# Attention and soft mixture of experts: the upper part of k by a transfer, epsilon and a running sum on ScalarE, halved casts, one routing step to a round

## The chip, the cores and the metric

The kernel runs on one core of a Trainium2 chip. The time is that of one execution on the device, in microseconds. It is the median of several runs; the profile is of one further execution.

## The reference

Attention for 8 batches of 12 heads (448 positions, 64 values per head), then a soft mixture of 8 experts with 4 slots each. Cut to what matters:

```python
scores = scale * np.matmul(q, k.transpose(0, 1, 3, 2))          # causal mask follows
scores = scores - np.max(scores, axis=-1, keepdims=True)
attn = np.exp(scores)
attn = attn / (np.sum(attn, axis=-1, keepdims=True) + 1e-09)
x = np.matmul(attn, v)                                            # then (3584, 768)
logits = x @ phi                                                  # (3584, 32)
d = np.exp(logits - logits.max(0)); d /= d.sum(0) + 1e-09         # over all tokens
slot_input = d.T @ x
slot_out[e] = np.maximum(slot_input[e] @ w1[e], 0.0) @ w2[e]
c = softmax(logits, over slots)
out = c @ slot_out
```

## The kernel before

The attention stage works in rounds, one per head: 96 rounds, two to a pair of heads, 12 to a batch (a block). Each round is software-pipelined. In round `i`, TensorE makes the scores of head `i+2` (`scores1`: matmuls `s<-tri` for the mask and `s<-qd,ks`), adds corrections and the negated row maximum to the scores of head `i` (`scores2`: `s<-r,k`), and multiplies the exponentials of head `i-1` by the values (`attv`: `po<-va,pt`). One `po` bank serves all heads; three banks hold scores.

q and k are held in two parts. `cast_k` and `cast_q` round the raw `qk` tile into `ks` and `qd` on ScalarE. `sub_k` and `sub_q` put the remainders into partitions 64 to 127 of `ks` and `r2` on GpSimd (`ks<-qk,ks`, `r<-qk,qd`). `copy_k2` copies the rounded (upper) part of k from partitions 0 to 63 of `ks` to partitions 64 to 127 of `k2`, which the corrections take as weights (`k<-ks` in the profile). The tiles `qd`, `ks`, `k2` and `r2` exist twice, for even and odd pairs.

The row maximum goes over several engines. ScalarE evacuates a piece of the scores (`max_evac`, `mx<-s`). VectorE takes the maximum with the rest, transposes and reduces (`mx<-s,mx`, `mt<-mx`, `r<-mt`). TensorE transposes the result (`rt<-ident,r`) into the one bank `m`, VectorE reduces it (`mr<-rt`), and GpSimd spreads it (`r<-mr`). ScalarE makes the exponentials (`exps`, `pt<-s`), which frees a bank of scores. `norm` divides: step 0 adds epsilon to the row sums (`sm<-po`), step 1 takes the reciprocal, step 2 multiplies (`x<-po,sm`), which frees `po`.

At the end of a round, `plan` runs a step of the routing, if there is one:

- `xtrans` transposes `x` of a pair (`xt<-ident,x`, copied out by ScalarE as `xts<-xt`).
- `next_logits` multiplies two pairs by `phi` (`g<-xts,phi`).
- `logits_e` transposes exponentials and logits (`tp`), copies them, and calls `logits_z`, which updates the running sum `run_z`.
- `dispatch` multiplies `x` by the exponentials (`sp<-x,gs`).

Each of these takes the same one bank `m` as `rt`. `logits_d` (`ld` in the table) makes the routing exponentials `gs` and the factor `al` on ScalarE, once a block.

The order within a round is written out by hand in `ORDER`, one list for even and one for odd rounds. Every engine works in the order of the program. Loads go out on SP's queue in program order, at the head of an odd round: k, v, q, and in every second pair a tile of expert weights. After attention come the expert stage and the combination, which run against the stream of expert weights.

Of the kernel before, what the change touches and what calls it, by code (L numbers as in the profile page):

```python
# [9 lines left out]
F32 = mybir.dt.float32  # L10
F32R = mybir.dt.float32r
BF16 = mybir.dt.bfloat16
AF = mybir.ActivationFunctionType
ALU = mybir.AluOpType
# [3 lines left out]
P = 128  # L18
NB, NH, S, HD = 8, 12, 448, 64
# [8 lines left out]
EPS = 1e-9  # L28
# [3 lines left out]
NR, XB = 2, 3  # L32
# [7 lines left out]


ORDER = (
# [4 lines left out]
)  # L47

SC0, SC1, SC2, SC3 = 512, 0, 320, 960
# [30 lines left out]
def attention_soft_moe(ctx: ExitStack, tc: tile.TileContext, qk, va, phi, w1, w2, out):  # L80
    nc = _Core(tc)
    const = ctx.enter_context(tc.tile_pool(name="const", bufs=1, side="left"))
# [27 lines left out]
    st = {}  # L110
# [54 lines left out]
    k2_, r2_ = ([t[k] for t in ops] for k in range(2))  # L165
    po0 = ps_1.tile([P, NCH, VC], F32, name="po")
    identb = const.tile([P, P], BF16, name="identb")
    nc.vector.tensor_copy(out=identb, in_=ident)
    for i in range(NR):
        nc.gpsimd.memset(r2_[i][0:64, :, :].bitcast(F32), 0.0)  # L170
# [5 lines left out]
    def misc(name):  # L176
        return ps_1.tile([P, 512], F32, tag="m", name=name)
# [9 lines left out]
    def cast_q(p, hs=slice(0, 2)):  # L187
        if p < NPAIR:
            nc.scalar.activation(out=qd_[p % NR][:, hs], in_=st["raw", 0, p][:, hs], func=AF.Copy)

    def cast_k(p, hs=slice(0, 2)):
        if p < NPAIR:
            nc.scalar.activation(out=ks_[p % NR][:, hs], in_=st["raw", 1, p][:, hs], func=AF.Copy)

    def sub_k(p, hs=slice(0, 2), eng=None):
        if p < NPAIR:
            ks = ks_[p % NR][64:P, hs]
            (eng or nc.gpsimd).tensor_tensor(out=ks, in0=st["raw", 1, p][64:P, hs], in1=ks, op=ALU.subtract)

    def copy_k2(p, hs=slice(0, 2)):  # L200
        if p < NPAIR:
            nc.scalar.activation(out=k2_[p % NR][64:P, hs], in_=ks_[p % NR][0:64, hs],
                                 func=AF.Copy)

    def sub_q(p, hs=slice(0, 2), eng=None):
        if p < NPAIR:
# [107 lines left out]
    def norm(i, k):  # L314
        if not 0 <= i < NHD:
            return
        p, h = divmod(i, 2)
        if k == 0:
            if i % 6 == 0:
                xn = x_[p // 3 % XB]  # L320
                st["xn", p // 3] = xn
                for k in range(3):
                    st["x", p + k] = xn[:, :, P * k:P * k + P]
            sm = st["sm", i] = moe.tile([P, NCH], F32, tag="sm", name=f"sm{i}", bufs=2)
            nc.vector.tensor_scalar(out=sm, in0=st.get(("po", i), po0)[:, :, HD], scalar1=EPS, scalar2=None, op0=ALU.add)
        elif k == 1:
            nc.vector.reciprocal(out=st["sm", i], in_=st["sm", i])
        else:
            sm = st.pop(("sm", i))
            nc.vector.tensor_tensor(out=st["x", p][:, :, HD * h:HD * h + HD], in0=st.get(("po", i), po0)[:, :, 0:HD],  # L330
                                    in1=sm.unsqueeze(2).to_broadcast([P, NCH, HD]), op=ALU.mult)
# [12 lines left out]
    def logits_a(b, js, g, first=True, last=True):  # L344

        for j in js:
            xt = st.pop(("xt", b * PPB + j))
            for c in range(NCH):
                nc.tensor.matmul(g[32 * c:32 * c + 32], phis[j // 3][:, j % 3], xt[:, P * c:P * c + P],
                                 start=first and j == js[0], stop=last and j == js[-1], skip_group_check=True)  # L350

    def logits_t(j, g):

        nc.vector.tensor_tensor(out=lt, in0=g, in1=lt if j else mk, op=ALU.add)
# [15 lines left out]
    def logits_z(b):  # L370
        nc.vector.scalar_tensor_tensor(out=run_z, in0=run_z, scalar=st["al", b][:, 0:1],
                                       in1=st.pop(("bs", b)), op0=ALU.mult, op1=ALU.add)

    def logits_e(b):
        tp = misc(f"tp{b}")
        nc.tensor.transpose(out=tp[:, 0:P], in_=gs, identity=ident)
        nc.tensor.transpose(out=tp[:, P:2 * P], in_=lt, identity=ident)
        st["dn", b] = gs.rearrange("p (c s) -> p c s", s=NSLOT)
        nc.scalar.activation(out=gs, in_=tp[:, 0:P], func=AF.Copy)
        nc.scalar.activation(out=lg[:, b], in_=tp[:, P:2 * P], func=AF.Copy)  # L380
        logits_z(b)

    def dispatch_a(b, hf, sp, sl=slice(0, 384)):
        dn = st["dn", b]
# [9 lines left out]
                                       op0=ALU.mult, op1=ALU.add)  # L394


    def first_logits(b, m):
        logits_a(b, (0, 1), m[:, 384:512], first=b == 0)
        logits_t(0, m[:, 384:512])

    def next_logits(b, j, m):
        logits_a(b, (j, j + 1), m[:, 0:P])
        logits_t(j, m[:, 0:P])

    def dispatch(b, hf):
        sp = misc(f"sp{b}_{hf}")
        dispatch_a(b, hf, sp)
        if hf:

            first_logits(b + 1, sp)  # L410
        dispatch_b(b, hf, sp)

    plan = {}
    for b in range(NB):
        o, last = 12 * b, b == NB - 1
        for j, r in enumerate((3, 5, 8, 9, 11, 13)):
            if not last or j < PPB - 2:
                plan[o + r] = lambda p=b * PPB + j: xtrans(p)
        plan[o + 10] = lambda b=b: next_logits(b, 2, misc(f"g{b}_2"))
        if not last:  # L420
            plan[o + 14] = lambda b=b: (next_logits(b, 4, misc(f"g{b}_4")), logits_b(b, lt))
            plan[o + 16] = lambda b=b: logits_e(b)
            plan[o + 18] = lambda b=b: dispatch(b, 0)
            plan[o + 19] = lambda b=b: dispatch(b, 1)
    plan[7] = lambda: first_logits(0, misc("g0_0"))


    warm(START[0])
# [57 lines left out]
    for i in range(NHD + 1):  # L486
        p, h = divmod(i, 2)
        if h:
            load_qk(p + 3, 1)
            if p + 1 < NPAIR - 1:  # L490
                loads_v(p + 1)
            load_qk(p + 3, 0)
            if p % 2 and nload < RES:
                load_w(nload)
                nload += 1
        if i == NHD - 3:

            loads_v(NPAIR - 1, nc.scalar)
        if i < 2:
            scores2(i, (1, 0, 2))  # L500
            if i:
                scores1_all(3)
                max_evac(3)
            scores2(i, (3,))
            exps(i)
            if i == 0:
                max_row(1, 0)
                max_row(1, 1)
                max_spread(1)
                sub_q(1, h1)  # L510

        qs = [int(n[1]) for n in ORDER[h] if n[0] == "a"]
        first = qs[:2] if qs[0] == 3 else qs[:1]
        for n in ORDER[h]:
            if i < 2 and (n in ("ev", "exp") or n[0] in "kt" or n in ("c0", "c3", "c12")):
                continue
            if i == 0 and n in ("mr0", "mr1", "sp"):
                continue
            if n[0] == "k" or n in ("c0", "c3", "c12"):
                scores1(i + 2, n)  # L520
            elif n[0] == "t":
                scores2(i, (int(n[1]),))
            elif n[0] == "a":
                attv(i - 1, (int(n[1]),), first)
            elif n[0] == "x":
                max_keys(i + 2, int(n[1]))
            elif n[0] == "n":
                norm(i - 1, int(n[1]))
            elif n in ("mr0", "mr1"):
                max_row(i + 1, int(n[2]))  # L530
            elif n == "ld":
                if i % 12 == 3 and i > 12:
                    logits_d(i // 12 - 1, lt)
            elif n == "plan":
                if later and i:
                    later.pop(0)()
                plan.get(i, int)()
            else:
                {"ev": lambda: max_evac(i + 2), "exp": lambda: exps(i), "sp": lambda: max_spread(i + 1),
                 "ck": lambda: cast_k(p + 2), "sk": lambda: sub_k(p + 2), "cq": lambda: cast_q(p + 2),  # L540
                 "c2": lambda: copy_k2(p + 1), "sq": lambda: sub_q(p + 2)}[n]()
        if i == NHD - 1:

            scs.close()
            pe = att.enter_context(tc.tile_pool(name="pe", bufs=1, space=PSUM, reuse_waits="tile"))
            ps = [pe.tile([P, 512], F32, name=f"e{k}") for k in range(6)]
            po = st["po", i] = ps[2][:, 0:NCH * VC].rearrange("p (c n) -> p c n", n=VC)
# [259 lines left out]
```

## Time and profile before

| | us |
|---|---|
| median of 3 runs | 463.79 (463.17 to 464.12) |
| profiled execution | 461.8, span 460.1 |
| TensorE matmul busy | 426.2 (93%) |
| VectorE busy | 354.2 (77%) |
| ScalarE busy | 329.7 (72%) |
| GpSimd busy | 266.1 (58%) |

Busy time is an average over the attention stage (to about 355 us) and the expert stage. In the rows of a timeline the first number is the start in microseconds from the start of the span, the second the time that the row covers; a row with `x10` merges ten neighbouring instructions. In rows of groups, the numbers behind `x47 |` are busy microseconds and the mean nanoseconds of one.

### The profile page before, as it was taken

How to read it: one execution, taken by the hardware profiler on the slowest of the kernel's cores; microseconds unless marked ns; L12 is line 12 of the kernel's file. 1: busy time of each engine (PE TensorE's matmuls, PEld its weight loads, DVE VectorE, ACT ScalarE, POOL GpSimd, SP SyncE). 2: the span in 40 equal slices, each digit the busy share in tenths (PEclk: the TensorE clock that was granted, in tenths of full speed). 3: DMA queues.
4: the chain of work that ended last, by engine and by line, in shares of the span. 5: the costliest groups of instructions: out<-in, count | busy, mean ns of one | idle time of the engine just before them, and what ended most of it. 6: DMA issues, size and time to landing. Idle time of an engine off the chain costs nothing.

```text
span 460.1 us, 12026 instructions
## 1 busy us (share of the span) xinstructions
PE 426.2 (93%) x4581; PEld 363.3 (79%) x4581; DVE 354.2 (77%) x1051; ACT 329.7 (72%) x489; POOL 266.1 (58%) x215
## 2 busy tenths in 40 slices
PE   7899999999999999999999999999999998996640
PEld 3799999999899989998999899999989754542220
DVE  5888899888988988898899888988897468422340
ACT  6798888889888979987889788888985211332230
POOL 5888788677778777877777687777772000000000
PEclk9999999999999999999999999999999999999985
DMA  7376666676567765776566766667648999999998
GB/s 267 112 273 236 222 205 219 225 234 219 191 205 255 234 211 173 236 251 217 192 209 217 233 234 206 214 215 236 227 158 285 374 407 413 416 414 414 401 395 301
DMA packets 38200, 119.03 MB, mean 259 GB/s; under 512 B 4096, under 2 KB 11776, under 8 KB 38144
## 3 DMA queue, kind: packets, MB, share of 16 engines
q1 hardware_dynamic: 38000, 118.01, 73.1%
q8 instruction: 36, 0.59, 0.5%
q10 hardware_dynamic: 144, 0.27, 0.1%
q14 instruction: 20, 0.16, 0.1%
HBM read 107.25 MB, written 11.01 MB: 257 GB/s over the span
## 4 chain that ended last, share of the span: by engine, by line
PE 68%; DMA 14%; DVE 6%; ACT 5%; issue 3%; POOL 1%; SPq 0%; ACTq 0%; POOLq 0%
PE po L64 29%; PE s L64 23%; DMA w<-in_w_dram 13%; PE xt L64 5%; PE sp L64 3%; PE g L64 2%; ACT pt L64 2%; PE rt L64 2%; ACT ks L64 2%; DVE mx L64 1%; PE e L64 1%; PE pp L64 1%; DMA qk<-in_qk_dram 1%; DVE run_z L64 1%; PE hp L64 1%
## 5 line engine op out<-in xcount | busy, mean ns | idle before, releaser
L64 PE MATMUL po<-va,pt 128*128 128x65 f32 x1900 | 193.5, 250 | 0.0
L64 PEld LDWEIGHTS po<-va,pt 128*128 128x128 f32 x1900 | 190.5, 171 | 0.3 <-DVE x L64 0.2
L64 DVE TENSOR_TENSOR mx<-s,mx 128x320 f32<-128x320 f32 (+2 forms) x288 | 100.8, 350 | 28.2 <-ACT mx L64 24.6
L64 POOL TENSOR_TENSOR r<-qk,qd 64x896 fp32r<-64x896 f32 (+1 forms) x50 | 101.4, 2028 | 6.6 <-ACT qd L64 2.8
L64 POOL TENSOR_SCALAR_AFFINE_SELECT r<-mr 14x448 fp32r<-14x448 f32 x96 | 61.4, 640 | 75.6 <-DVE mr L64 67.6
L64 ACT ACTIVATE pt<-s 128x1024 f32<-128x1024 f32 x96 | 98.0, 1021 | 7.4 <-PE s L64 3.8
L64 POOL TENSOR_TENSOR ks<-qk,ks 64x896 fp32r<-64x896 f32 (+1 forms) x47 | 98.0, 2085 | 5.1 <-ACT ks L64 1.5
L64 PE MATMUL s<-r,k 128*128 128x320 f32 (+3 forms) x384 | 83.1, 298 | 1.8 <-POOL r L64 1.7
L64 PE MATMUL s<-qd,ks 128*128 128x448 f32 (+3 forms) x384 | 77.3, 312 | 1.1 <-DVE ks L64 1.1
L64 ACT ACTIVATE mx<-s 128x448 f32<-128x448 f32 x96 | 52.4, 546 | 34.5 <-PE s L64 17.3
L64 PEld LDWEIGHTS s<-r,k 128*128 128x128 f32 (+1 forms) x384 | 60.0, 176 | 5.9 <-POOL r L64 2.2
L64 DVE STREAM_TRANSPOSE mt<-mx 128x448 f32<-128x448 f32 x96 | 61.9, 645 | 3.3
L64 DVE TENSOR_REDUCE r<-mt 128x14 f32<-128x448 f32 x96 | 58.5, 609 | 0.1
L64 PEld LDWEIGHTS s<-qd,ks 128*128 128x128 f32 (+1 forms) x384 | 55.8, 182 | 2.6 <-ACT qd L64 1.8
L64 ACT ACTIVATE ks<-qk 128x896 fp32r<-128x896 f32 (+1 forms) x50 | 45.6, 914 | 2.8 <-DMA qk<-in_qk_dram 2.8
L64 ACT ACTIVATE k<-ks 64x896 fp32r<-64x896 f32 (+1 forms) x49 | 45.8, 934 | 1.1
L64 ACT ACTIVATE qd<-qk 128x896 fp32r<-128x896 f32 (+1 forms) x50 | 46.1, 922 | 0.4 <-DMA qk<-in_qk_dram 0.3
L64 PEld LDWEIGHTS <-identb 128*128 128x128 bf16 x320 | 29.5, 102 | 18.5 <-issue 14.8
L64 DVE TENSOR_TENSOR x<-po,sm 128x256 f32<-128x256 f32 x95 | 40.3, 425 | 3.3
L64 PE MATMUL s<-tri,identb 128*128 128x64 bf16 (+2 forms) x288 | 40.0, 235 | 0.9
L64 ACT ACTIVATE xts<-xt 128x512 f32<-128x512 f32 x47 | 28.1, 598 | 9.0 <-PE xt L64 6.0
L64 PE MATMUL so<-w,ht 128*32 128x384 f32 x256 | 24.9, 492 | 6.9 <-DMA w<-in_w_dram 5.2
(126 smaller groups left out, 398.1 us busy)
## 6 DMA issues: line engine op xcount, KB each, us to landing
w<-in_w_dram SPq DMA_DIRECT2D x64, 768.0 KB, 8.0
qk<-in_qk_dram SPq DMA_DIRECT2D x94, 448.0 KB, 3.4
va<-in_va_dram SPq DMA_DIRECT2D x47, 260.0 KB, 3.4
out_dram<-ot SPq DMA_DIRECT2D x28, 384.0 KB, 6.7
qk<-in_qk_dram SPq DMA_DIRECT2D x4, 224.0 KB, 3.6
va<-in_va_dram ACTq DMA_DIRECT2D x1, 260.0 KB, 4.8
phi<-in_phi_dram SPq DMA_DIRECT2D x2, 48.0 KB, 3.8
```

Source lines behind the costliest of these rows:

```text
L64: return self._tc.keep_in_program_order(op(*args, **kwargs))
```

## The change

- `copy_k2` becomes a transfer from SBUF to SBUF on SP's queue, except for the first pair, and moves from the end of an odd round to the head of the next even one in the list, where it serves the pair `p + 1` a round earlier.
- Step 0 of `norm` and the update of `run_z` run on ScalarE.
- k and q are cast by single heads: k in the even round (one head at its head, one before the exponential), q in the odd round (before, both heads of both were cast in the even round).
- The first logits of a block leave the second dispatch and become a step of their own at round 8; some transposes move by a round.

```diff
-    ("c3", ..., "t3", "ck",
-     "mr0", "exp", "x0", "a2", "mr1", "x2", "x3", "a1", "cq", "sp", "n0", ...),
-    ("c3", ..., "a3", "exp", "mr0", ..., "sq", "c2", "x4", "plan"),
+    ("c2", "ck0", "c3", ..., "t3", "ck1",
+     "mr0", "exp", "x0", "a2", "mr1", "x2", "x3", "a1", "sp", "n0", ...),
+    ("cq0", "c3", ..., "a3", "cq1", "exp", "mr0", ..., "sq", "x4", "plan"),
...
+    eps = const.tile([P, 1], F32, name="eps")
+    nc.gpsimd.memset(eps, EPS)
...
+            if p < 1:
+                nc.scalar.activation(out=k2_[p % NR][64:P, hs], in_=ks_[p % NR][0:64, hs],
+                                     func=AF.Copy)
+            else:
+                nc.sync.dma_start(out=k2_[p % NR][64:P, hs].bitcast(F32),
+                                  in_=ks_[p % NR][0:64, hs].bitcast(F32))
...
-            nc.vector.tensor_scalar(out=sm, in0=st.get(("po", i), po0)[:, :, HD], scalar1=EPS, ...)
+            nc.scalar.activation(out=sm, in_=st.get(("po", i), po0)[:, :, HD], func=AF.Identity, bias=eps[:, 0:1])
...
-        logits_z(b)
+        nc.scalar.activation(out=run_z, in_=run_z, func=AF.Identity, scale=st["al", b][:, 0:1],
+                             bias=st.pop(("bs", b))[:, 0:1])
...
         dispatch_a(b, hf, sp)
-        if hf:
-
-            first_logits(b + 1, sp)
         dispatch_b(b, hf, sp)
...
-        for j, r in enumerate((3, 5, 8, 9, 11, 13)):
+        for j, r in enumerate((3, 5, 9, 10, 12, 13)):
...
-        plan[o + 10] = lambda b=b: next_logits(b, 2, misc(f"g{b}_2"))
+        for j, r in ((0, 8), (2, 11)):
+            plan[o + r] = lambda b=b, j=j: next_logits(b, j, misc(f"g{b}_{j}"))
...
-    plan[7] = lambda: first_logits(0, misc("g0_0"))
```

ScalarE, an even round with a transposed pair at its start, in the fifth block. `k_125` is `k2`, `qk_25` the raw tiles of pair 25, `mx` the evacuation and `pt` the exponential. Before:

```order
L64 ACTIVATE pt_87<-s_2443 128x1024
L64 ACTIVATE k_125<-ks_122 64x896
L64 ACTIVATE xts_2599<-xt_2594 128x512
L64 ACTIVATE mx<-s_2601 128x448
L64 ACTIVATE ks_122<-qk_25_2548 128x896
L64 ACTIVATE pt_85<-s_2499 128x1024
L64 ACTIVATE qd_121<-qk_25_2551 128x896
```

Now:

```order
L64 ACTIVATE pt_87<-s_2491 128x1024
L64 ACTIVATE sm_2631<-po,eps 128x4
L64 ACTIVATE xts_2643<-xt_2638 128x512
L64 ACTIVATE ks_122<-qk_25_2591 128x448
L64 ACTIVATE mx<-s_2647 128x448
L64 ACTIVATE ks_122<-qk_25_2591 128x448
L64 ACTIVATE pt_85<-s_2540 128x1024
L64 ACTIVATE sm_2681<-po,eps 128x4
```

The copy of k is gone ahead of `xts`, the epsilon has come there, one half of the cast of k stands ahead of `mx`, and the cast of q is no longer in this round.

TensorE, from the second dispatch of a block (`sp_1`) to the end of the round after it. Before, with the first logits behind the dispatch and a transpose in the next round:

```order
L64 MATMUL sp_1_2484<-x_91,gs 32x384 x4
L64 MATMUL sp_1_2484<-xts_2285,phi_221 32x128 x4
L64 MATMUL sp_1_2484<-xts_2386,phi_221 32x128 x4
L64 LDWEIGHTS identb
L64 MATMUL s_2499<-tri,identb 128x64
```

```order
L64 MATMUL rt_2519<-ident,r_2482 14x128
L64 MATMUL po<-va_86,pt_87 128x65 x5
L64 MATMUL xt_2541<-ident,x_90 128x128 x4
L64 LDWEIGHTS identb
L64 MATMUL s_2553<-tri,identb 128x64
```

Now, the end of that next round:

```order
L64 MATMUL rt_2560<-ident,r_2530 14x128
L64 MATMUL po<-va_86,pt_87 128x65 x5
L64 MATMUL g_0_2581<-xts_2329,phi_223 32x128 x4
L64 MATMUL g_0_2581<-xts_2432,phi_223 32x128 x4
L64 LDWEIGHTS identb
L64 MATMUL s_2597<-tri,identb 128x64
```

The logits stand in a round of their own, and the transposes follow a round later.

SP's queue, now (`k_125` is `k2`, `va` the values, `w` a tile of expert weights):

```order
L64 DMA qk_12_1200<-in_qk_dram 128x896
L64 DMA w_1202<-in_w_dram 128x1536
L64 DMA k_125<-ks_122 64x896
L64 DMA qk_13_1305<-in_qk_dram 128x896
L64 DMA va_86<-in_va_dram 128x520
L64 DMA qk_13_1308<-in_qk_dram 128x896
```

The transfer is new in its third row; the other rows stand as before.

More of the change, by code (lines that the diff above doesn't have):

```diff
@@ L201, in copy_k2 @@
         if p < NPAIR:
-            nc.scalar.activation(out=k2_[p % NR][64:P, hs], in_=ks_[p % NR][0:64, hs],
-                                 func=AF.Copy)
+            if p < 1:
[4 more added lines that the diff above has]
+                                  in_=ks_[p % NR][0:64, hs].bitcast(F32))
     def sub_q(p, hs=slice(0, 2), eng=None):
@@ L324, in norm @@
             sm = st["sm", i] = moe.tile([P, NCH], F32, tag="sm", name=f"sm{i}", bufs=2)
-            nc.vector.tensor_scalar(out=sm, in0=st.get(("po", i), po0)[:, :, HD], scalar1=EPS, scalar2=None, op0=ALU.add)
+            nc.scalar.activation(out=sm, in_=st.get(("po", i), po0)[:, :, HD], func=AF.Identity, bias=eps[:, 0:1])
         elif k == 1:
@@ L394, in dispatch_b @@
                                        op0=ALU.mult, op1=ALU.add)
-    def first_logits(b, m):
-        logits_a(b, (0, 1), m[:, 384:512], first=b == 0)
-        logits_t(0, m[:, 384:512])
     def next_logits(b, j, m):
@@ L539, in attention_soft_moe @@
                 {"ev": lambda: max_evac(i + 2), "exp": lambda: exps(i), "sp": lambda: max_spread(i + 1),
-                 "ck": lambda: cast_k(p + 2), "sk": lambda: sub_k(p + 2), "cq": lambda: cast_q(p + 2),
+                 "ck0": lambda: cast_k(p + 2, h0), "ck1": lambda: cast_k(p + 2, h1), "sk": lambda: sub_k(p + 2),
+                 "cq0": lambda: cast_q(p + 2, h0), "cq1": lambda: cast_q(p + 2, h1),
                  "c2": lambda: copy_k2(p + 1), "sq": lambda: sub_q(p + 2)}[n]()
```

8 rows, old and new, of the table ORDER are left out of this document.

## The prediction

> **What bounds the kernel now.** I read the page first, then the chain of waits, then the timeline of TensorE between 180 and 217 us, where every kind of round occurs.
>
> ```profile
> span 460.1 us, 12026 instructions
> ...
> PE 68%; DMA 14%; DVE 6%; ACT 5%; issue 3%; POOL 1%; SPq 0%; ACTq 0%; POOLq 0%
> ```
>
> TensorE holds 68% of the chain. That doesn't mean that it never stalls, since matmul ends are modelled. So I compare starts of the same stretch in two rounds. Round 48 has no routing step (a "plain" round), round 49 has four transposes `xt`.
>
> ```profile
> 186.72 1.23 PE L64 MATMUL po<-va,pt 128*128 128x65 f32 x10
> ...
> 188.05 0.24 PE L64 MATMUL s<-tri,identb 128*128 128x64 bf16 x2
> ...
> 190.03 1.23 PE L64 MATMUL po<-va,pt 128*128 128x65 f32 x10
> ...
> 191.10 0.60 PE L64 MATMUL xt<-ident,x 128*128 128x128 f32 x4
> ...
> 191.54 0.25 PE L64 MATMUL s<-tri,identb 128*128 128x64 bf16 x2
> ```
>
> Ten `po` matmuls take 191.10 - 190.03 = 1.07 us start to start, and four transposes 0.44. In the plain round the next work (`s<-tri`, first of the next scores) begins 188.05 - 186.72 = 1.33 after the first `po`: 0.26 us of waiting. The chain of waits names the cause, the exponential `pt`, which ends at 188.00 and must free the bank that the new scores take:
>
> ```profile
> 186.98 1.02 ACT pt L64
> ...
> 317.88 1.02 ACT pt L64
> ```
>
> These two rows are 130.9 us apart, three blocks of 12 rounds: a block is 43.6 us, and its one plain round is where ScalarE is late. There are seven such blocks. Two more waits come once in each block. In round 51 the copy `k<-ks` of the upper part of k sits behind the routing exponentials and ends at 199.36, and the correction matmuls of round 52 wait for it. In round 53, VectorE's `run_z` delays the reduction `mr`, which must empty the bank that `xt` needs:
>
> ```profile
> 198.41 0.95 ACT L64 ACTIVATE k<-ks 64x896 fp32r<-64x896 f32 x1
> ...
> 198.73 0.25 PE L64 MATMUL s<-tri,identb 128*128 128x64 bf16 x2
> ...
> 200.04 0.81 PE L64 MATMUL po<-va,pt 128*128 128x65 f32 x10
> ...
> 203.49 0.94 DVE L64 SCALAR_TENSOR_TENSOR run_z<-run_z,al,bs 128x1 f32<-128x1 f32 x1
> ...
> 204.19 1.23 PE L64 MATMUL po<-va,pt 128*128 128x65 f32 x10
> ...
> 205.14 0.27 DVE L64 TENSOR_REDUCE mr<-rt 14x32 f32<-14x128 f32 x1
> ...
> 205.96 0.25 PE L64 MATMUL s<-tri,identb 128*128 128x64 bf16 x2
> ```
>
> From 204.19 to 205.96 is 1.77, against 191.54 - 190.03 = 1.51 undisturbed: 0.26 us lost. For the other wait, the undisturbed round stands in the next fence (an even round with `xts` at its start), which also gives the margins that the new order uses up.
>
> ```profile
> 191.36 0.12 DVE L64 TENSOR_SCALAR sm<-po 128x4 f32<-128x4 f32 x1
> ...
> 191.73 0.42 DVE L64 TENSOR_TENSOR x<-po,sm 128x256 f32<-128x256 f32 x1
> 191.74 0.60 ACT L64 ACTIVATE xts<-xt 128x512 f32<-128x512 f32 x1
> ...
> 192.22 0.65 PE L64 MATMUL s<-r,k 128*128 128x448 f32 x3
> 192.47 0.55 ACT L64 ACTIVATE mx<-s 128x448 f32<-128x448 f32 x1
> ...
> 192.71 0.81 PE L64 MATMUL po<-va,pt 128*128 128x65 f32 x10
> 192.91 0.94 ACT L64 ACTIVATE ks<-qk 128x896 fp32r<-128x896 f32 x1
> ...
> 193.05 0.88 DVE L64 TENSOR_TENSOR mx<-s,mx 128x192 f32<-128x192 f32 x2 [0.38 <-ACT mx L64]
> ...
> 193.85 0.27 DVE L64 TENSOR_REDUCE mr<-rt 14x32 f32<-14x128 f32 x1
> ```
>
> From `s<-tri` to `po` is 192.71 - 191.54 = 1.17 here and 200.04 - 198.73 = 1.31 in round 52: 0.14 us lost to the copy.
>
> **The change part by part.** Only what TensorE waits for moves the end, and the tail of expert weights follows the attention stage by the same amount.
>
> *Copy of k by a transfer.*
>
> ```profile
> qk<-in_qk_dram SPq DMA_DIRECT2D x94, 448.0 KB, 3.4
> ```
> ```profile
> 186.79 0.33 SPq L64 DMA_DIRECT2D qk<-in_qk_dram  x1
> ```
> ```profile
> L64 ACT ACTIVATE k<-ks 64x896 fp32r<-64x896 f32 x47 | 44.6, 949 | 1.1
> ...
> L64 ACT ACTIVATE qd<-qk 128x448 fp32r<-128x448 f32 x4 | 2.3, 574 | 0.1
> ...
> L64 ACT ACTIVATE al<-run_m,run_m 128x1 f32<-128x1 f32 x8 | 2.3, 282 | 0.0
> ```
>
> ScalarE loses 0.949 us per pair, and the 0.14 wait in seven blocks goes: gain 0.14. The transfer moves 64 rows of 3584 bytes, half of a `qk` load. The trace has no transfer from SBUF to SBUF. From below it costs nothing; from above I take a whole load, 3.4 us. On SP it stands ahead of the k load, which was issued at 186.79 in this cycle; it needs only the earlier corrections done, so it goes out no later than that load, and lands by 190.2. The correction matmuls that read it start at 192.22, so 2.0 us are spare. I take nothing, nearest to a load of half the size. The load behind it lands at 186.79 + 3.4 = 190.2 as well, and the half cast that now opens the round can't start before the epsilon is done (191.36 + 0.28 = 191.64): 1.4 us of cover, and half a load is at most 1.7 us if it shared everything with it. The cost if that cover goes is ScalarE standing still ahead of `mx`.
>
> *Half casts.* Two halves take 2 x 0.574 = 1.15 instead of some 0.95 (the k copy has as many columns), 0.2 us more for each of k and q, off TensorE's path by themselves. In an even round only one half now lies between `mx` and `pt`, so the exponential comes about 0.4 us earlier. That alone covers the 0.26 of the plain round. It also is no longer plain: the diff puts the last `xt` there, so TensorE has 0.44 us of work before it wants the bank. Gain 0.26. The other half stands at the head of the round, behind `xts` where there is one (six of twelve rounds). ScalarE's neighbours overlap by 0.1 (`ks<-qk` begins at 192.91, `mx` ends at 193.02). So `xts`, from 191.74, lets the next one start 0.5 later, and the half cast the one after it 0.47 later: `mx` at 192.71 instead of 192.47, 0.24 late. Is that covered? `mr` ended at 193.85 + 0.27 = 194.12. The next routing step would at the earliest come 1.07 after the `po` row of 193.50 (next fence), at 194.57, and handing over took 0.05: 0.40 us of cover. So nothing, as long as it stays under 0.40.
>
> *Epsilon on ScalarE.*
>
> ```profile
> L64 DVE TENSOR_SCALAR sm<-po 128x4 f32<-128x4 f32 x95 | 11.8, 124 | 2.7 <-PE po L64 2.7
> ```
>
> Nearest on ScalarE is `al`, also with a bias per partition: 0.282. VectorE loses 0.124, but its reciprocal now waits 0.282 plus a hand-over, so `x` ends about 0.2 later: 191.73 + 0.42 + 0.2 = 192.35, against `po` at 192.71 that needs the bank. Nothing, except at the very end, where it is in line: +0.16. ScalarE's total is even: per pair -0.95 + 2 x 0.28 + 0.4. Bounds for one epsilon on the path: from -0.12 (VectorE alone is freed) to +0.28.
>
> Queued behind it on ScalarE is what counts. It waits for the last `po`, so nothing after it can begin before that. Only one place suffers, round 51 with its routing exponentials:
>
> ```profile
> 197.73 0.39 ACT L64 ACTIVATE gs<-lt,run_m 128x128 f32<-128x128 f32 x1
> ...
> 198.28 0.60 PE L64 MATMUL xt<-ident,x 128*128 128x128 f32 x4
> ```
>
> `gs` started at 197.73. The last `po` is done some 0.26 after `xt` starts (191.36 - 191.10), at 198.54, and the epsilon takes about 0.2 more: `gs` 1.0 later. The k copy (0.95) is gone from behind it, a half cast (0.47 in sequence) has come: `mx` of round 52 is 0.4 to 0.5 late, at or past the cover of 0.40. Bounds 0 to 0.3; I take 0.10.
>
> *`run_z` on ScalarE.* VectorE loses 0.94 ahead of `mr`: gain 0.26 of the wait. On ScalarE it stands ahead of `mx` of round 53, together with two copies, a half cast and the epsilon; that makes `mx` some 0.35 late, under the 0.40.
>
> *Routing steps one to a round.* The first logits of a block leave the second dispatch and get a round.
>
> ```profile
> 193.50 1.23 PE L64 MATMUL po<-va,pt 128*128 128x65 f32 x10
> ...
> 194.66 0.64 PE L64 MATMUL g<-xts,phi 128*32 128x128 f32 x16
> ...
> 195.23 0.26 PE L64 MATMUL s<-tri,identb 128*128 128x64 bf16 x2
> ```
> ```profile
> 209.06 0.85 PE L64 MATMUL sp<-x,gs 128*32 128x384 f32 x8
> ...
> 209.85 0.26 PE L64 MATMUL s<-tri,identb 128*128 128x64 bf16 x2
> ...
> 213.00 0.85 PE L64 MATMUL sp<-x,gs 128*32 128x384 f32 x8
> ...
> 214.22 0.26 PE L64 MATMUL s<-tri,identb 128*128 128x64 bf16 x2
> ```
>
> Inside the dispatch they cost (214.22 - 213.00) - (209.85 - 209.06) = 0.43. Alone they cost 195.23 - 193.50 - 1.07 = 0.66. So +0.23: TensorE pays for the separate step, and that nearly uses up the plain round.
>
> **Sum.** Per block -0.26 - 0.14 - 0.26 + 0.23 + 0.10 = -0.33, times seven -2.3. The first block has two more plain even rounds, of which the late `mx` leaves about 0.1 each: -0.2. The end: +0.16. Total -2.3 us. The profiled execution took 461.8 us (span 460.1), 2.0 under the median of 463.79; the change set against the median gives 461.5, 0.5% less.
>
> **Rivals.** (1) *Slower: ScalarE's queue ahead of `mx` becomes the bound.* Epsilon, `xts` and half cast now all stand there. It decides once `mx` is over 0.40 us late in rounds with `xts`; six rounds in seven blocks are 42, so each 0.1 us past that point costs 4.2 us. At 0.5 late it gives 461.5 + 4.2 = 465.7. For it: ScalarE has no idle time left there, and the epsilon at its head waits for `po`. Against: 0.24 by the rows. The Trainium skill, "ScalarE: Activation LUTs", section "Rules for kernel authors", advises additions on VectorE rather than on ScalarE; by that rule this edit is a loss, and this rival is the form in which it would show here. The rows agree on the single price (0.28 against 0.12) and leave it off TensorE's path. 17%.
> (2) *No change.* The late `mx` of rounds 52 and 53 costs 0.3 rather than 0.1, and the wait behind `run_z` only moves to ScalarE (0.1 gained, not 0.26): the sum per block is +0.03, total about 0 to -0.8: 463.3. For it: ScalarE takes over just what VectorE gives up, in the block's fullest rounds. 21%.
> (3) *More.* The new stall is nothing and the earlier k frees other small waits: per block -0.45, total -3.6: 460.2. 18%.
> (4) *The transfer is late.* It collides with weight loads, and TensorE waits at the corrections or ScalarE at the half cast; half a microsecond in a third of 48 pairs is +8, less the gain: 469. Against: the 2.0 and 1.4 us of cover. 3%.
>
> **How the numbers follow.** My forecast has 41%. A measurement of this kernel can tell about 0.2%, 0.93 us, from no change: the forecast and (3) lie beyond it, 0.59; (2) within, 0.21; (1) and (4) are slower, 0.20. The range reaches down a little below (3), 459.9, and up to (1), 465.7, leaving out the worse half of (1), (4) and the rim of (3). The faster cases alone run from 459.9 to 462.8.
>
> **What would show.** Right: no `ACT pt` of 1.02 in the chain once a block; `xt` after `po` at 1.07 in round 53; `s<-tri` to `po` at 1.17 in round 52; `mx` some 0.24 after its place in rounds with `xts`, without a later start of the next routing step; SP's copy of k landing more than 1 us ahead of its reader. Wrong: `xt`, `g` or `tp` starting later than 1.07 (1.16 for `g`) after `po` with `mr` just ahead of it, in many rounds; ScalarE idle ahead of `ks<-qk` until a transfer lands; an `ACT_TABLE_LOAD` more than now.

## The result and the profile after

| | before | after |
|---|---|---|
| median, us | 463.48 (461.83 to 464.62, 6 runs) | 469.14 (468.11 to 472.07, 6 runs) |
| ratio | 1 | 1.0143 (1.0121 to 1.0164) |
| profiled execution, us | 461.8, span 460.1 | 468.11, span 466.3 |

The change makes the kernel 1.4% slower. The page of after answers to the rows shown of before as follows (span and instructions; the share of the chain by engine; the load queue's packets, megabytes and share of the 16 DMA engines; DMA issues with the median time from issue to landing):

```profile
span 466.3 us, 12351 instructions
...
q1 hardware_dynamic: 41760, 128.79, 85.2%
...
PE 42%; DMA 21%; POOL 17%; DVE 7%; issue 6%; ACT 3%; SPq 0%; POOLq 0%; ACTq 0%; DVEq 0%
...
qk<-in_qk_dram SPq DMA_DIRECT2D x94, 448.0 KB, 4.7
va<-in_va_dram SPq DMA_DIRECT2D x47, 260.0 KB, 4.4
k<-ks SPq DMA_DIRECT2D x47, 224.0 KB, 6.4
```

For comparison, the queue and the values' load on the page of before:

```profile
q1 hardware_dynamic: 38000, 118.01, 73.1%
...
va<-in_va_dram SPq DMA_DIRECT2D x47, 260.0 KB, 3.4
```

The transfer of 224 KB lands 6.4 us after its issue, later than a load of twice the bytes. The loads around it now land after 4.7 and 4.4 us, where they took 3.4. The queue moves 9% more bytes (128.79 against 118.01) and holds the engines for 18% more time (85.2% of 466.3 against 73.1% of 460.1). TensorE's share of the chain falls from 68% to 42%, and DMA's and GpSimd's rise.

Who waits shows in the list of waits (total us, times, longest). After, then before:

```profile
ACT ks L64 <- DMA qk<-in_qk_dram: 9.0, 12, 1.6
...
ACT qd L64 <- DMA qk<-in_qk_dram: 3.1, 7, 1.2
...
PE s L64 <- DMA k<-ks: 0.6, 2, 0.4
```

```profile
ACT ks L64 <- DMA qk<-in_qk_dram: 2.8, 2, 1.4
```

ScalarE stands still ahead of the casts until a load lands, 19 times in these rows instead of twice. TensorE waits for the transfer itself only twice. One place with both, in the fifth block, as the timeline of after has it (a row's bracket is the engine's idle time before it and what ended it):

```profile
185.20 0.92 SPq L64 DMA_DIRECT2D w<-in_w_dram  x1
...
186.16 0.47 SPq L64 DMA_DIRECT2D k<-ks  x1
...
188.17 0.33 SPq L64 DMA_DIRECT2D qk<-in_qk_dram  x1
...
194.39 0.70 PE L64 MATMUL s<-r,k 128*128 128x448 f32 x3 [0.42 <-DMA k<-ks]
...
195.54 0.58 ACT L64 ACTIVATE ks<-qk 128x448 fp32r<-128x448 f32 x1 [1.61 <-DMA qk<-in_qk_dram]
...
196.02 0.53 ACT L64 ACTIVATE mx<-s 128x448 f32<-128x448 f32 x1
...
196.58 0.88 DVE L64 TENSOR_TENSOR mx<-s,mx 128x192 f32<-128x192 f32 x2 [2.16 <-ACT mx L64]
...
197.70 0.64 PE L64 MATMUL g<-xts,phi 128*32 128x128 f32 x16 [0.76 <-DVE mr L64]
```

The chain of waits has the load's own time, and ahead of it the remainder on GpSimd that frees the raw tile for the load:

```profile
186.03 2.12 POOL r L64
...
188.17 7.29 DMA qk<-in_qk_dram
```

The k load behind the transfer lands 7.29 us after its issue. The half cast at the round's head waits 1.61 us for it. Behind that cast on ScalarE stands `mx`; VectorE's maximum, `mr` and finally TensorE's routing step come late in turn: 0.76 us. The transfer itself, issued 8.2 us ahead, is late for its reader by 0.42. GpSimd's larger share of the chain comes from here: a load is issued when the remainder `r<-qk,qd` is done, so once the load's time is on the chain, the remainder ahead of it is too.

Ahead of the transfer and the k load, the queue has a tile of expert weights (768 KB, issued at 185.20). That is so in each of the ten waits ahead of the half cast of k after the first 30 us, which are 6.3 of the 9.0 us: the load waited for was issued 3.0 to 3.6 us behind such a tile. Loads of q and k between 40 and 340 us that were in flight beside a tile of weights land after 4.8 us (median of 48), the others after 4.0 (33); on the trace of before it is 3.4 and 3.3. So the k load gets late enough to be waited for where the transfer meets a tile of weights. No run moved the weights, so what that would be worth is not shown.

By windows over the fifth block, the end of each row is the granted clock, the DMA share and GB/s. Before, after, and the fully loaded stretch of after in which that load is under way:

```profile
168.16:211.73 43.57, 43.43 (x477) 40.59 (x476) 38.72 (x117) 37.95 (x54) 32.93 (x24) 1.00 0.67 219
```

```profile
169.60:214.94 45.34, 43.92 (x477) 40.63 (x476) 36.55 (x104) 35.86 (x73) 33.10 (x25) 1.00 0.83 241
...
191.67:195.50 3.83, 3.41 (x35) 3.16 (x34) 2.57 (x8) 1.90 (x4) 2.74 (x2) 1.00 1.00 291
```

The granted clock is 1.00 in all three. The DMA engines go from 67% busy to 83% for 10% more throughput, and around 193 us they are full. By the starts of `rt` in the same round, the six blocks from round 20 to 92 take 265.44 us instead of 261.76 (+3.7), and rounds 2 to 20 take 65.61 instead of 63.16 (+2.4).

### The profile page after: what moved, and what is told of

It reads as the page before. It is cut to its first block, busy times and chain, and to the rows that moved or that the text cites. A ratio compares the mean times of both kernels' runs of the same rounds, so it can differ in the third digit from the quotient of the medians.

```text
span 466.3 us, 12351 instructions
## 1 busy us (share of the span) xinstructions
PE 425.3 (91%) x4581; PEld 362.3 (78%) x4581; DVE 338.6 (73%) x948; ACT 315.8 (68%) x637; POOL 266.2 (57%) x216
## 3 DMA queue, kind: packets, MB, share of 16 engines
q1 hardware_dynamic: 41760, 128.79, 85.2%
## 4 chain that ended last, share of the span: by engine, by line
PE 42%; DMA 21%; POOL 17%; DVE 7%; issue 6%; ACT 3%; SPq 0%; POOLq 0%; ACTq 0%; DVEq 0%
PE po L64 19%; PE s L64 13%; POOL r L64 12%; DMA qk<-in_qk_dram 10%; DMA w<-in_w_dram 6%; POOL ks L64 5%; DMA out_dram<-ot 4%; PE xt L64 2%; PE sp L64 2%; PE g L64 2%; DVE mx L64 1%; PE e L64 1%; PE rt L64 1%; PE hp L64 1%; DVE lm L64 1%
## 5 line engine op out<-in xcount | busy, mean ns | idle before, releaser
L64 PE MATMUL s<-qd,ks 128*128 128x448 f32 (+3 forms) x384 | 76.1, 309 | 1.6 <-ACT qd L64 1.4
L64 ACT ACTIVATE ks<-qk 128x448 fp32r<-128x448 f32 x96 | 54.7, 571 | 10.7 <-DMA qk<-in_qk_dram 9.0
L64 ACT ACTIVATE qd<-qk 128x448 fp32r<-128x448 f32 x96 | 54.9, 573 | 4.1 <-DMA qk<-in_qk_dram 3.1
L64 PEld LDWEIGHTS <-identb 128*128 128x128 bf16 x320 | 28.2, 100 | 20.2 <-issue 16.6
L64 ACT ACTIVATE sm<-po,eps 128x4 f32<-128x4 f32 x95 | 25.0, 264 | 17.9 <-PE po L64 15.5
```

The source lines that it names most:

```text
L64: return self._tc.keep_in_program_order(op(*args, **kwargs))
```

## The experiments

Theory T: the transfer is the loss; it holds the DMA engines longer than its bytes say, the loads land late, and the cast at the head of the round exposes that. Rival Q: ScalarE's queue ahead of `mx` is the bound (the prediction's first rival). Each time is beside the kernel before, on the same chip.

**The change without the copy.** From the third pair on nothing writes the upper part of k.

```diff
-            if p < 1:
+            if p < 2:
                 nc.scalar.activation(out=k2_..., in_=ks_..., func=AF.Copy)
-            else:
-                nc.sync.dma_start(...)
```

> The changed kernel with no copy of k after the first two pairs (left out: every later pair uses an old upper part of k). Theory T (the transfers slow the loads behind them on the queue, and ScalarE, which now opens a round with a half cast, stands still until k lands): 460.5 us, 0.6% under the kernel before, and no wait of ScalarE for a load in mid-kernel. Rival Q (the epsilon and the half cast ahead of the evacuation mx make ScalarE late by themselves): stays at 468 to 469.

461.76 us against 462.5; ratio 0.9992 (0.9962 to 1.0022). Its page and its list of waits:

```profile
qk<-in_qk_dram SPq DMA_DIRECT2D x94, 448.0 KB, 3.4
```

```profile
ACT ks L64 <- DMA qk<-in_qk_dram: 2.5, 2, 1.4
```

Loads and waits are those of before again; five of the six blocks from round 20 on take 43.29 to 43.33 us, where before takes 43.6. Q falls: everything else that was put on ScalarE is still there. T had the time at 460.5, 0.6% under before, and that did not come: in total this kernel is not measurably faster. Its start is part of that (below).

**The transfer alone.** The kernel before, with the copy as a transfer at the head of the even round, and the casts as they were.

```diff
-    ("c3", ..., 
+    ("c2", "c3", ...,
-    ("c3", ..., "n2", "sq", "c2", "x4", "plan"),
+    ("c3", ..., "n2", "sq", "x4", "plan"),
...
+            if p < 1: (ScalarE) else: nc.sync.dma_start(...)
```

> The kernel before with the copy of k as the transfer alone, at the head of the even round; casts, epsilon, run_z and routing as before. T: the cast of k comes some 1.4 us later in the round here, so fewer late loads show: 464 to 467, loads still landing 4.5 us or more after issue. If the late loads need no half cast to hurt: 468 to 470. Q: 462.5, since only the wait for the copy in round 52 of each block is gone.

465.15 against 462.5; 1.0055 (1.0023 to 1.0087). From its page, then its waits:

```profile
qk<-in_qk_dram SPq DMA_DIRECT2D x94, 448.0 KB, 4.5
...
k<-ks SPq DMA_DIRECT2D x47, 224.0 KB, 6.6
```

```profile
ACT qd L64 <- DMA qk<-in_qk_dram: 13.2, 18, 2.1
```

The same landing times stand here without any other part of the change, so it is the transfer that lengthens the loads. But the loss is under half of the change's: with both casts behind `mx`, much of the waiting falls where ScalarE has time, as the next run shows.

**The casts back behind the evacuation.** The change, with both half casts of k behind `mx`.

```diff
-    ("c2", "ck0", "c3", ..., "t3", "ck1",
+    ("c2", "c3", ..., "t3", "ck0", "ck1",
```

> The changed kernel, transfer included, with both half casts of k behind the evacuation, where the whole cast stood. If the late load hurts because the half cast opens the round: 462 to 465, near the transfer alone (1.0055 of before). If the transfers hurt wherever the cast is: 468 to 470.

465.3 against 462.77; 1.005 (1.0023 to 1.0077). The landing times stay (4.5 and 6.5), the waits for loads are as many in time:

```profile
ACT qd L64 <- DMA qk<-in_qk_dram: 7.9, 11, 1.5
ACT ks L64 <- DMA qk<-in_qk_dram: 5.9, 6, 1.5
```

13.8 us of waiting here against 12.1 in the change, and yet 0.9% less loss. So the length of the wait is not what costs. What costs is that `mx`, and with it the whole row maximum, comes late behind it. The 7.9 us are ahead of the half cast of q, which stands at the head of the odd round with `mx` behind it as well, and yet `mx` can be on time (timeline of this run):

```profile
196.01 0.26 PE L64 MATMUL s<-tri,identb 128*128 128x64 bf16 x2
...
196.48 0.58 ACT L64 ACTIVATE qd<-qk 128x448 fp32r<-128x448 f32 x1 [0.67 <-DMA qk<-in_qk_dram]
...
196.96 0.54 ACT L64 ACTIVATE mx<-s 128x448 f32<-128x448 f32 x1
```

`mx` begins 0.95 us after `s<-tri` here, where the kernel before has 0.93 without a wait. Behind these eleven waits it begins 0.94 to 1.75 us after `s<-tri`; behind the change's ten waits ahead of the half cast of k it begins 1.43 to 2.89 us after it. Why the load of q is late by less was not tested.

**The transfer behind the k load.** If the load suffers by standing behind the transfer, let the transfer go second.

```diff
-    ("c2", "ck0", "c3", ...
+    ("ck0", "c3", ...
...
             load_qk(p + 3, 1)
+            copy_k2(p + 1)
```

> The changed kernel with the transfer issued behind the load of k instead of ahead of it. T: the load of k lands at 3.4 us again, while the transfer still has some 4 us to its reader: 461 to 464. If the transfer slows whatever shares the engines with it, ahead or behind: 466 to 469. Q: 468 to 469.

481.75; 1.0438 (1.0371 to 1.0505): a miss. Its waits:

```profile
ACT ks L64 <- DMA k<-ks: 14.3, 16, 2.4
PE s L64 <- DMA k<-ks: 11.7, 12, 2.4
```

The load is hardly waited for any more; the transfer is, twice over. T's landing after 3.4 us did not come either: the loads land after 4.5 us here too, so the order on the queue does not spare them. TensorE needs its result, and the next cast may not overwrite `ks` before the transfer has read it. The transfer still lands 5.3 us after its issue, so it has no room for 2 us of delay. In this profile the granted clock was also 0.51 over two windows of 6.9 us (from 35.6 and from 264.3), so the waits are not the whole of the 4.4%.

**Is it bytes, the source, or the partitions?** Four kernels add an unread transfer to the kernel without the copy, in the place of the transfer: the same bytes from HBM to 128 partitions; the same bytes from SBUF to 128 partitions; 0.68 of the bytes (608 columns) from HBM to partitions 64 to 127; the same 0.68 from partitions 0 to 63 of SBUF to 64 to 127.

```diff
+            else:
+                nc.sync.dma_start(out=dum, in_=qk[p, :, 1, 0])                       # HBM, 128
...
+                nc.sync.dma_start(out=dum, in_=ks_[p % NR][:, 0].bitcast(F32))       # SBUF, 128
...
+                nc.sync.dma_start(out=dum[64:P], in_=qk[p, 0:64, 1]...[:, 0:608])    # HBM, 64
...
+                nc.sync.dma_start(out=dum[64:P], in_=ks_[p % NR][0:64]...[:, 0:608]) # SBUF, 64
```

> As the kernel with no copy of k, plus a load that nobody reads in the transfer's place: as many bytes, from HBM to all 128 partitions (448 elements each). If the bytes on the queue are the cause: 467 to 469. If it is the transfer's own kind (SBUF to SBUF, 64 partitions to the other 64) that makes it slow: 460.5 to 462.5. Q: 468 to 469.

> No copy of k after the first two pairs; in the transfer's place one that nobody reads, from SBUF to SBUF over all 128 partitions (448 elements each, the transfer's bytes). If the SBUF source makes a transfer slow: loads of q and k land after 4.3 us or more, this transfer after 6, and the time is 466 to 469. If the 64 partitions do: loads at 3.5, 461 to 463.

> The same, but the unread transfer loads from HBM into partitions 64 to 127 alone (608 elements each, 0.68 of the bytes). If writing 64 partitions makes a transfer slow: loads land after 4 us or more, 464 to 468. If the SBUF source does: 3.4 to 3.6, 461 to 463.

> The same, but the unread transfer goes from partitions 0 to 63 to partitions 64 to 127 of SBUF (608 elements each): the changed kernel's own kind with 0.68 of its bytes, without a reader in TensorE. By either cause: loads land after 4 us or more, and 464 to 468; if only the waiting reader hurts: 461 to 463.

The times were 462.28, 462.82, 464.32 and 468.64 us. The first is what was expected if the bytes are harmless. The second has the time of a harmless source and the third that of slow partitions, at its lower edge, but in both the loads land after 3.8 us, between the two readings. The last lies a little above its range. From the pages of the four in this order, the queue; that of the kernel without a copy stands first:

```profile
q1 hardware_dynamic: 38000, 118.01, 74.3%
```

```profile
q1 hardware_dynamic: 44624, 128.56, 79.4%
```

```profile
q1 hardware_dynamic: 44624, 128.56, 80.8%
```

```profile
q1 hardware_dynamic: 41680, 125.17, 79.0%
```

```profile
q1 hardware_dynamic: 41680, 125.17, 80.4%
```

The share times the span is the time per DMA engine that the queue's packets took. Less that of the kernel without a copy (74.3% of 462.0 = 343.3 us), divided by the number of transfers, it gives a price, in which a slower pace of the neighbours' packets is contained:

| kernel | span, us | engine time of one, us | per 224 KB | `qk` lands after | ratio to before |
|---|---|---|---|---|---|
| no copy | 462.0 | | | 3.4 | 0.9992 (0.9962 to 1.0022) |
| HBM, 128 partitions | 461.8 | 0.51 | 0.51 | 3.5 | 0.9996 (0.9971 to 1.0022) |
| SBUF, 128 partitions | 462.0 | 0.65 | 0.65 | 3.8 | 0.9989 (0.9954 to 1.0025) |
| HBM, 64 partitions | 462.7 | 0.48 | 0.71 | 3.8 | 1.0031 (0.9997 to 1.0066) |
| SBUF, 64 to 64 partitions | 465.4 | 0.67 | 0.99 | 4.0 | 1.0114 (1.0032 to 1.0195) |
| the change | 466.3 | 1.15 | 1.15 | 4.7 | 1.0143 (1.0121 to 1.0164) |

The base of these prices scatters: for the same loads the queue held the engines 336.3 us in the kernel before and 343.3 here, which is 0.15 us a transfer. The bytes as such are harmless. A source in SBUF and a target of 64 partitions together nearly double the price, which is clear of the scatter, and only then does the time rise beyond doubt (two runs, so its interval is wide). For each of the two alone the larger price (0.65 and 0.71 against 0.51) is not clear of it. The packets say more, since those of the unread transfers have a size of their own. Between 60 and 340 us, packets of 1792 bytes to 128 partitions took 76 ns in the mean from HBM and 74 from SBUF; packets of 2432 bytes to 64 partitions took 124 and 126, which is a fifth to a quarter more per byte. So the 64 partitions lengthen the transfer's own packets and the source in SBUF does not. Nothing reads what the last transfer brings; its loss is by the loads that it holds up. Its waits:

```profile
ACT ks L64 <- DMA qk<-in_qk_dram: 7.4, 8, 1.5
```

**The copy on GpSimd.** The page has GpSimd busy for 57% of the span. First by heads behind each remainder, then ahead of the spreading at the head of each round, then the same with ScalarE copying the first six pairs.

```diff
-                nc.sync.dma_start(...)
+                nc.gpsimd.tensor_copy(out=k2_[p % NR][64:P, hs], in_=ks_[p % NR][0:64, hs])
-    ("c2", "ck0", "c3", ..., "n0", "sk", "n1", ...
+    ("ck0", "c3", ..., "n0", "sk", "c20", "n1", ...          # first; "c21" behind "sq" in odd rounds
+    ("c20", "ck0", "c3", ...   and   ("c21", "cq0", "c3", ... # second and third
...
-            if p < 1:
+            if p < 6:                                         # third
```

> The changed kernel with the copy of k on GpSimd, by single heads, behind each remainder. All else of the change stays, and the corrections have what they need: 460.5 to 462 if a half copy takes some 0.6 us in GpSimd's idle time (it waits 0.45 to 0.9 us for the row maximum in each round); 465 or more if a half copy takes over 1 us and the spreading of the maximum comes late.

494.07; 1.0662 (1.0603 to 1.0722): far above the expected range. A half copy takes 0.553 us, but it stands behind the remainder (2.1 us), and the next cast must not overwrite `ks` before it is done. Its waits:

```profile
ACT ks L64 <- POOL k L64: 48.7, 45, 3.1
```

> The changed kernel with the copy of k on GpSimd by single heads, now ahead of the spreading of the maximum, where GpSimd idles 0.45 to 0.9 us a round; one half copy takes 0.55. The half cast that waited for it in the run before has a round more. T: blocks of 43.3 to 43.5 us and 460.5 to 462. If the spreading comes late even so: 465 or more.

469.72 against 462.77; 1.0148 (1.0115 to 1.0182). From round 20 on the blocks are those of a kernel without any copy (43.31 to 43.33 us in five of the six), so the copy can be had off ScalarE and off the queue. But rounds 2 to 20 take 73.9 us instead of 63.2. Its timeline there, and a window with the granted clock third from the end:

```profile
44.26 0.77 POOL L64 TENSOR_SCALAR_AFFINE_SELECT sid<-sid 128x32 f32<-128x32 f32 x3
...
45.72 0.64 POOL L64 TENSOR_SCALAR_AFFINE_SELECT r<-mr 14x448 fp32r<-14x448 f32 x1
...
46.41 1.22 PE L64 MATMUL s<-r,k 128*128 128x448 f32 x3 [2.75 <-POOL r L64]
```

```profile
50.00:56.00 6.00, 6.00 (x46) 5.38 (x46) 2.47 (x7) 2.76 (x5) 2.92 (x3) 0.50 0.59 184
```

GpSimd still builds its tables (`sid`) in these rounds; the spreading `r<-mr` comes behind them and behind the copies, TensorE waits 2.75 us, and in the stretch behind that wait the granted clock is 0.50. The trace has it at 0.50 from 46.0 to 56.2 us, which alone is up to 5.1 of the 10.7 us.

> The copy of k on GpSimd ahead of the spreading, as in the run before, but ScalarE copies the first six pairs by single heads. Theory S (GpSimd's queue carries its set-up work in the first ten rounds, and the copies make it late there alone: 2.75 us of waiting of TensorE for the spreading at 46.4 us, and a granted clock of 0.5 behind it): blocks stay at 43.3 us, rounds 2 to 20 take about 63 us instead of 73.9, and the time falls to 460 to 463. Rival (GpSimd with copies is late in any block's fullest rounds): the loss stays, 468 to 470. Third: ScalarE cannot carry the copies in the first block, a stall there of some tenths in several rounds: 463 to 465.

463.81 against 462.56; 1.0035 (1.0013 to 1.0057): rounds 2 to 20 take 66.2 us and the six blocks 260.24. The cause of the 10.7 us is thus the start, as expected, for 7.7 of them; up to 5.1 of these are the low clock, which this profile does not have (1.00 throughout the attention stage), and the medians of the two kernels differ by 5.9. Of the 3.0 us that remain, 2.3 are the third reading, that ScalarE cannot carry the copies in the first block: TensorE waits once for `qd` (0.88) and twice for `pt` (0.69 each; timeline):

```profile
19.54 0.21 PE L64 MATMUL s<-qd,ks 128*64 128x64 f32 x1 [0.88 <-ACT qd L64]
...
37.94 0.24 PE L64 MATMUL s<-tri,identb 128*128 128x64 bf16 x2 [0.69 <-ACT pt L64]
```

**The routing steps and the running sum alone.** The kernel before, with only the steps one to a round and `run_z` on ScalarE; no transfer, no epsilon on ScalarE, no half casts.

```diff
-        logits_z(b)
+        nc.scalar.activation(out=run_z, in_=run_z, func=AF.Identity, scale=..., bias=...)
...
-        if hf:
-            first_logits(b + 1, sp)
...
-        for j, r in enumerate((3, 5, 8, 9, 11, 13)):
+        for j, r in enumerate((3, 5, 9, 10, 12, 13)):
...
+        for j, r in ((0, 8), (2, 11)):
```

> The kernel before with two parts alone: routing steps one to a round, and run_z on ScalarE. k is still copied by ScalarE, epsilon is on VectorE, casts are whole. By the prediction's terms per block: -0.26 (plain round filled) + 0.23 (own step) - 0.26 (run_z), no stall of the epsilon's kind: -0.29 a block, -2.0 in all, 0.4% faster. If run_z on ScalarE only moves the wait: no change.

460.87 (459.33 to 462.97) against 462.77; 0.9964 (0.9944 to 0.9985), the fastest of all. Its blocks take 43.32 us each, all six within 0.01. The whole gain of the change in these blocks is in this part. It beats both kernels, the one before by 0.4%.

## Why the prediction was wrong

**The step that failed** is the transfer's price: "I take nothing, nearest to a load of half the size", with 3.4 us as its upper end, and what was built on it, that the load behind it lands at "186.79 + 3.4 = 190.2 as well". The transfer landed after 6.4 us, outside those bounds, and the load behind it no longer after 3.4 but after 4.7 at the median and 7.29 at worst. The assumption beneath was that a transfer is priced by its bytes like a load. In DMA engine time, the slowing of its neighbours included, it costs 1.15 us against 0.51 for the same bytes from HBM to all partitions.

Of the two covers, one gave way. The transfer goes out 9.0 us ahead of its reader (median of 47), and in 42 of 47 pairs lands more than 1 us ahead of it; TensorE waits for it twice, 0.6 us in all. The 1.4 us ahead of the half cast were measured from a load that lands after 3.4 us. They suffice for the median load and not for the ten that land after 5.7 to 7.29, for which ScalarE waits 6.3 us.

The Trainium skill, "SBUF — State Buffer", section "Door 1: The DMA port swizzle", says that partitions 0 to 63 reach only one half of the 16 DMA ports and 64 to 127 the other, and its section "The DMA setup-cost knee" advises transfers of 128 partitions. The runs agree in direction: packets to 64 partitions took a fifth to a quarter longer per byte, and the price per 224 KB is 0.99 against 0.65 within SBUF. No row here shows the ports themselves, and the rule does not tell why the loads beside such a transfer from SBUF come late.

**The outcome was rival (4)**, "the transfer is late", at its price (469), by both ways that it named: TensorE waiting at the corrections (0.42 at 194.39) and ScalarE at the half cast (1.61 at 195.54). The second is the main one, as the run with later casts shows, and the collision with weight loads that it named stands at each of the ten waits. That the price met the time so closely is in part luck: it was half a microsecond in sixteen pairs, and the trace has ten waits of 0.63 us in the mean. I gave it 3% because I held two covers against it that both rested on the one guessed duration. "ScalarE idle ahead of `ks<-qk` until a transfer lands" was among the signs of being wrong, and it is what the list of waits shows.

**Rival (1)**, ScalarE's queue, is excluded by the run without a copy. The late `mx` came as worked out: in a round with `xts` where no load is late, the timeline of after has

```profile
189.63 0.25 PE L64 MATMUL s<-tri,identb 128*128 128x64 bf16 x2
...
189.83 0.60 ACT L64 ACTIVATE xts<-xt 128x512 f32<-128x512 f32 x1 [0.18 <-PE xt L64]
...
190.79 0.54 ACT L64 ACTIVATE mx<-s 128x448 f32<-128x448 f32 x1
...
191.62 1.23 PE L64 MATMUL po<-va,pt 128*128 128x65 f32 x10
...
192.69 0.60 PE L64 MATMUL xt<-ident,x 128*128 128x128 f32 x4
```

`mx` 1.16 us after `s<-tri` instead of 0.93 (192.47 - 191.54), so 0.23 late for 0.24 predicted; and `xt` comes 1.07 after the `po` row of 191.62, without a stall. Epsilon takes 0.264 us, for which I had used 0.282:

```profile
L64 ACT ACTIVATE sm<-po,eps 128x4 f32<-128x4 f32 x95 | 25.0, 264 | 17.9 <-PE po L64 15.5
```

**The sum of a block held**: -0.33 us predicted; 43.29 to 43.33 us in five of six blocks without the copy, against 43.6, so about -0.3. The exponential `pt` no longer stands in the chain of after once a block. What the routing steps and `run_z` give alone is -0.30, for -0.26 (plain round) -0.26 (`run_z`) +0.23 (separate step) = -0.29. So the copy of k, the epsilon and the half casts, which were to give -0.14 + 0.10 together, gave next to nothing even with the copy left out.

Two side sums were off, without bearing on the outcome. Rival (2)'s +0.03 a block, with the first block and the end, gives +0.2 in all and not 0 to -0.8; rival (3)'s -0.45 gives -3.2 and not -3.6.

**The first block was wrong too.** I predicted -0.2. There the first logits move from round 7 to 8, and that step had covered GpSimd's tables ahead of a spreading. In round 8 TensorE now waits about 0.7 us, whether there is a transfer or not; the row of after:

```profile
41.22 0.73 PE L64 MATMUL s<-r,k 128*128 128x448 f32 x3 [0.59 <-POOL r L64]
```

By starts the loss there is 0.75 us in the change, 0.78 without a copy and 0.64 in the fastest kernel. In the fastest kernel rounds 2 to 20 take 63.34 us against 63.16 before, so the gain of 0.2 did not come. In the six blocks the kernel without a copy gains 1.5 us and the fastest 1.8; their medians lie 0.7 and 1.9 under those of before. That the start makes this difference is likely and not shown.

**What stays open.** Of the 0.67 us of the unread transfer from 64 to 64 partitions, 0.50 are its own packets; the rest would be the slowing of its neighbours, about as large as the scatter of the base. The changed kernel's transfer has packets of the loads' own size, so how its 1.15 us divide is not known, nor why loads suffer more beside a transfer within SBUF. The runs with 0.68 of the bytes are scaled by bytes, which was not tried with the full size. Whether a transfer that keeps clear of the weights would cost nothing was not tried.

## What to carry to other kernels

A transfer with no like in the trace is not bounded by a load of more bytes: where nothing shows its kind, let the upper end lie beyond the nearest row, and give covers that hang on the same guess one chance of failing together, not two. A load's landing time is a resource that other instructions share. Look at what stands behind its reader on the engine and how soon that is due: with the half cast of k ahead of the evacuation the kernel lost 1.4%, with it behind 0.5%, at as much waiting in all. Look also at what else is on the queue just then, such as a tile of weights in every second pair. When an order is changed, go through the first block by itself, where one-off work lies in the queues.

## What the runs showed of the hardware

- A transfer of 224 KB from partitions 0 to 63 of SBUF to 64 to 127 landed after 6.4 us (median of 47) where a load of 448 KB took 3.4 without it and 4.7 with it. At a DMA share of 0.83, throughput was only 241 GB/s, while the kernel with the unread HBM load had 250 GB/s at a share of 0.75 in the same block:

```profile
169.18:212.85 43.67, 43.52 (x477) 40.57 (x476) 36.90 (x104) 36.15 (x74) 32.97 (x24) 1.00 0.75 250
```

- In the run without a copy the granted clock was 0.50 for 6.8 us near the start, about 3.4 us of work at full speed:

```profile
16.30:23.10 6.80, 6.80 (x43) 6.71 (x42) 4.29 (x11) 4.13 (x8) 5.02 (x4) 0.50 0.15 41
```

  The profiles of before and after have 1.00 in the same stretch. Why it falls in some executions, these runs don't tell.
- A copy of 64 x 448 on GpSimd takes 0.553 us, the mean of 94 in the first kernel with the copy there, about as long as ScalarE's casts of as many columns (0.574).
